# Reading x from two halves of a row in turns in a float32r up projection, with the output stored in two transfers

## The chip, the cores and the metric

The kernel runs on one core of a Trainium2 chip. The metric is the device time of one execution in microseconds; the time before is the median of three runs.

A core has a matrix engine (TensorE, PE in the profile; the loads of its stationary operand are listed as PEld), a vector engine (VectorE, DVE), an engine for activation functions (ScalarE, ACT), a general one (GpSimd, POOL) and SyncE (SP), which here issues nearly all DMAs. SBUF is the working memory, in 128 partitions; the matrix engine writes into PSUM.

## The reference

The first part is an mLSTM cell over 4 batches, 8 heads, 768 time steps and a head dimension of 40; the second a feed-forward block with the exact gelu on its output.

```python
for t in range(S):
    m_new = np.maximum(f_gate[:, :, t] + m, i_gate[:, :, t])
    f_stab = np.exp(f_gate[:, :, t] + m - m_new)
    i_stab = np.exp(i_gate[:, :, t] - m_new)
    m = m_new
    C = f_stab[:, :, None, None] * C + i_stab[:, :, None, None] * np.einsum('bhd,bhe->bhde', vt, kt)
    n = f_stab[:, :, None] * n + i_stab[:, :, None] * kt
    h_tilde = np.einsum('bhde,bhe->bhd', C, qt)
    denom = np.maximum(np.abs(np.einsum('bhd,bhd->bh', n, qt)[:, :, None]), 1.0)
    y[:, :, t] = h_tilde / denom / (1.0 + np.exp(-o_gate[:, :, t]))
x = y.transpose(0, 2, 1, 3).reshape(B * S, H * D)      # 3072 tokens x 320
h = x @ w_in                                           # 320 x 2048
g = 0.5 * h * (1.0 + erf(h / np.sqrt(2.0)))
out = g @ w_out                                        # 2048 x 320, 3072 rows
```

## The kernel before

**Chunks.** Time is cut into six chunks of 128 steps (`L`), and one chunk of all four batches makes 512 tokens (`TG`). For each chunk the class `Cell` computes the mLSTM output of each batch, and the feed-forward block follows: an up projection (`up_step` for chunk 0, `up` for chunks 1 to 5), the gelu, and a down projection (`first_down_steps`, `down_steps`). The down projection of chunk c is interleaved by hand with the cell of chunk c + 1: the strings `FRONT` and `DOWN` list the steps, a letter each, and `play` runs them in this order; the last chunk has no cell beside it. In `DOWN` an F is one piece of the down projection, X is `turn_y` and R is `split_x`.

**x.** `turn_y` transposes a finished batch into a PSUM tile px: 128 partitions by three groups (`NX + 1`) of 128 tokens. Groups 0 and 1 hold 128 features each; group 2 holds the last 64 features twice, once in each half of the partitions. For chunks 1 to 5 the projection is made in float32r (`F32R`) as three products, and x is stored as three parts: x_hi on ScalarE (L687), x_lo and x_all on VectorE in `split_x` (L700, L701). Each part is a tile of 128 partitions by three rows of 512 tokens, batch after batch; the 128 tokens of a batch stand in order in each row (`t`, a slice of 128 in all three rows).

**The up projection of chunks 1 to 5.** `up` has two rounds. Each round has two calls of `pair` and then `rest`. A `pair` makes 24 matmuls at L841: three products, two column blocks, two halves of the hidden width, two groups of features. The weights are the stationary operand (128 x 128), and one row of x, 128 partitions by 512 tokens, is the moving one; the result is a PSUM bank pu of 128 x 512. `rest` (L852) adds the last 64 features: 24 matmuls of 64 rows, whose two halves `e` use the upper and the lower 64 rows of the array. A chunk has so 96 matmuls of L841 and 48 of L852. ScalarE makes the gelu of each bank (L856) into `g.t`. Chunk 0 does the same in plain float32 with 256 columns (L786, L792).

**The down projection.** For chunks 1 to 5, `down_steps` uses a seven-product scheme on two halves of the tokens and of the hidden width; `hidden_sums` makes the sums it needs. Its matmuls (L922) have 128 tokens of one batch as the stationary operand, so the tokens of a batch come out as the partitions of a PSUM tile and of the output tile `o_sb`, in the order in which they stand in x.

**The stores.** `send` (L889) stores 128 rows of 320 float32 values of one batch with one DMA on SyncE. In a chunk of `down_steps`, `p3` sends batches 0 and 1, `p4` batches 2 and 3; in the last chunk `p4` runs for each of its two tiles by itself. SyncE's other transfers, the loads of q, k, v, the gates, M and the blocks of the next chunk, stand in the same queue in the order of the program.

Of the kernel before, what the change touches and what calls it, by code (L numbers as in the profile page):

```python
# [13 lines left out]
AF = mybir.ActivationFunctionType  # L14
OP = mybir.AluOpType

P = 128

I23 = 2.0 ** 23
PART = 1.0 - 2.0 ** -13  # L20
BASE = 1.0 + 2.0 ** -12
# [21 lines left out]
def kernel(  # L43
# [16 lines left out]
    nc = tc.nc  # L60

    B, H, S, D = q.shape
    L = P
    NCH = S // L
# [8 lines left out]
    R = P // 2  # L73
    NX = 2
# [59 lines left out]
    halves = (slice(0, R), slice(R, P))  # L134
# [8 lines left out]
    def load(n, first=0, end=4):  # L143

        if n >= NCH * B:
            return
        c, b = divmod(n, B)
        for src, dst in ((q, qb), (k, kb), (v, vb), (o_gate, None))[first:end]:
            if dst and swapped(c, b):
                x, to = src[b, :, c * L:(c + 1) * L, :].rearrange("h p d -> p h d"), dst[turn_of(n)][:, :, 0:D]  # L150
                for i in range(2):
                    nc.sync.dma_start(out=to[halves[i]], in_=x[halves[1 - i]])
                continue
            nc.sync.dma_start(out=dst[turn_of(n)][:, :, 0:D] if dst else out_of(n),  # L154
                              in_=src[b, :, c * L:(c + 1) * L, :].rearrange("h p d -> p h d"))
# [57 lines left out]
    a = gates.tile([BH, NCH, L], F32, name="a")  # L213
# [183 lines left out]
    def unread(bank):  # L397
        for _ in range(idle[0]):
            nc.tensor.matmul(bank, ident, ident, start=True, stop=True, skip_group_check=True)
        idle[0] = 0  # L400
# [3 lines left out]

    later_loads = []

    class Cell:


# [258 lines left out]
        def turn_y(self, b):  # L668
            n, t = self.c * B + b, slice(b * L, (b + 1) * L)
            if self.c > 0:  # L670
                px = ps_tr.tile([P, NX + 1, L], F32, name="px", tag="tr")
            else:
                px = ps_mm.tile([P, NX + 1, L], F32, name="px", tag="b")
            unread(px[:, 0, :])
            for k in range(NX + 1):
                y = ob[n % NLD][:, k * P:(k + 1) * P] if k < NX else y_rest.rearrange("p two r -> p (two r)")
                nc.tensor.transpose(px[:, k, :], y, ident)  # L677
            self.turned.append(b)
            if len(self.finished) > len(self.turned):
                self.twice(b + 1)  # L680
            if self.c == 0:
                nc.scalar.copy(out=first_x[:, :, t], in_=px)
                return
            self.px[b] = px
            if "x" not in parts:
                parts["x"] = raw.tile([P, NX + 1, TG], F32R, name="x_hi", tag="x", bufs=1)
            nc.scalar.activation(out=parts["x"][:, :, t], in_=px, func=AF.Copy, scale=PART)  # L687
            if self.c == 1 and b < NQ:
                load(n + NLD, 1, 3)
            if self.c == 1:  # L690
                load(n + NLD, 3, 4)
            else:
                later_loads.append(lambda: load(n + NLD, 3, 4))

        def split_x(self, b):
            px, t = self.px.pop(b), slice(b * L, (b + 1) * L)
            if b == 0:
                parts["x_lo"] = fars[0].tile([P, NX + 1, TG], F32R, name="x_lo", tag="x_lo", bufs=1)
            hi = parts["x"][:, :, t]
            nc.vector.scalar_tensor_tensor(out=parts["x_lo"][:, :, t], in0=px, scalar=-1.0 / BASE, in1=hi, op0=OP.mult, op1=OP.add)  # L700
            nc.vector.tensor_tensor(out=parts["x_all"][:, :, t], in0=px, in1=hi, op=OP.subtract)  # L701


    HF, HT, HD = NF // 2, TG // 2, DM // 2
# [9 lines left out]
    w_sums, parts, fars, w_hi, w_lo, w_mid = [], {}, [], [], [], {}  # L714
# [10 lines left out]
    def split_weight():  # L725
        i = len(w_lo)
        if i in (0, 3, 5, 8):
            two = shared([P, NX, 2, WP // 2], F32R, "w_in_hi")
            w_hi.extend([two[:, 0], two[:, 1]])
        elif i == 2:  # L730
            two = shared([P, 2, 2, WP // 2], F32R, "w_rest_hi")
            w_hi.append(two[:, 0])
            rest_two.append(two[:, 1])
        elif i == 7:
            w_hi.append(rest_two[0])
        w = w_all[i]
        nc.scalar.activation(out=w_hi[i], in_=w, func=AF.Copy, scale=PART * 2.0 ** -12)
        w_lo.append(w_f(F32R, "w_in_lo"))
        nc.vector.scalar_tensor_tensor(out=w_lo[i], in0=w_hi[i], scalar=-BASE * 2.0 ** 12, in1=w, op0=OP.mult, op1=OP.add)
# [3 lines left out]
    def join_weight(i):  # L743
        w_mid[i] = raw.tile([P, 2, WP // 2], F32R, name="w_in_mid", tag="pow") if i % 5 in (1, 4) else w_f(F32R, "w_mid")
        nc.vector.tensor_tensor(out=w_mid[i], in0=w_hi[i], in1=w_lo[i], op=OP.add)  # L745
# [74 lines left out]
    def up(g, sums_too, turns):  # L820

        def split_to(i):
            while len(w_lo) <= i:
                split_weight()

        def pair(f, ahead):

            at = [f // 2 * 5 + f % 2 * 3 + x for x in range(NX)]
            split_to(at[1])
            for i in at:  # L830
                if i not in w_mid:
                    join_weight(i)
            pus = [[pool.tile([P, TG], F32, name="pu", tag=tag) for e in range(2)]
                   for pool, tag in (((ps_h, "h"), (ps_mm, "a")), ((ps_tr, "tr"), (ps_mm, "b")))[f % 2]]
            ahead()
            mid = [w_mid.pop(i) for i in at]
            for n, (w, x) in enumerate((([w_hi[i] for i in at], parts["x"]), ([w_lo[i] for i in at], parts["x_lo"]), (mid, parts["x_all"]))):
                for i in range(2):
                    for e in range(2):
                        for k in range(NX):  # L840
                            nc.tensor.matmul(pus[i][e], w[k][:, e, i * P:(i + 1) * P], x[:, k, :],  # L841
                                             start=(n == 0 and k == 0), stop=False, skip_group_check=True)
            return pus

        def rest(u, banks, order):
            mid = w_mid.pop(5 * u + 2)
            for i in order:
                pu = banks[i]
                for n, (w, x) in enumerate(((w_hi[5 * u + 2], parts["x"]), (w_lo[5 * u + 2], parts["x_lo"]), (mid, parts["x_all"]))):
                    for e in range(2):  # L850
                        r = halves[e]
                        nc.tensor.matmul(pu[e], w[r, i // 2, i % 2 * P:(i % 2 + 1) * P], x[r, NX, :], start=False,  # L852
                                         stop=(n == 2), skip_group_check=True)

        def out(i, e, pu):
            nc.scalar.activation(out=g.t[:, HF * e + i, :], in_=pu[e], func=AF.Gelu, scale=4097.0)  # L856

        if c == 1:
            copy_chunk(2, range(1, B))
        b0 = pair(0, lambda: split_to(4))  # L860
        b1 = pair(1, lambda: join_weight(2))
        for step in turns[:1]:
            step()
        while later_loads:
            later_loads.pop(0)()
        if c == 1:
            copy_chunk(3)
        rest(0, b0 + b1, (0, 1, 2, 3))
        split_to(6)
        join_weight(5)  # L870
        join_weight(6)
        for i, pu in enumerate(b0 + b1):
            for e in range(2):
                out(i, e, pu)
        for step in sums_too[:5]:
            step()
        b2 = pair(2, lambda: split_to(9))
        hidden_sums(g, 0, 2)
        b3 = pair(3, lambda: (hidden_sums(g, 2, 4), join_weight(7)))
        for step in turns[1:] + sums_too[5:]:  # L880
            step()
        rest(1, b2 + b3, (2, 3, 0, 1))
        for i, e in ((2, 0), (2, 1), (3, 0), (0, 0), (1, 0), (3, 1), (0, 1), (1, 1)):
            out(4 + i, e, (b2 + b3)[i])
        hidden_sums(g, HF - 2, HF)
        hidden_sums(g, HF - 4, HF - 2)

    def send(c, b, o_sb):
        nc.sync.dma_start(out=out[b * S + c * L:b * S + (c + 1) * L, :], in_=o_sb)  # L889

    def first_down_steps(g):
        po = []
# [16 lines left out]
    def down_steps(c, g):  # L909
# [50 lines left out]
        def p3(pb):  # L960
            add(block(0, 1), pb, block(1, 0))
            for t in range(2):
                send(c, t, o_sb[0][:, t, :])
# [88 lines left out]
```

## Time and profile before

| | |
|---|---|
| time, median of 3 runs | 476.85 us (476.43 to 477.3) |
| span of the profiled execution, first to last instruction | 474.4 us |
| its own time beside the span | only the span is listed; it is 2.4 us under the median of the runs |
| PE busy, share of the span | 465.1 us, 98% |
| PEld, DVE, ACT, POOL busy | 403.4, 315.4, 238.2, 78.2 us |
| mean granted clock of TensorE | 1.000 |
| L841 in the chain that ended last | 24% |
| L852 in the chain that ended last | 6% |
| L922 in the chain that ended last | 33% |
| output stores (L889) | 24 of 160 KB, 1.9 us from issue to landing |

The busy time of PE is modelled from pipelined matmuls, each of which is listed longer than the distance to the next: L841's are listed at 387 to 633 ns. What one costs is read from the distance of their starts, or from a piece of the chain divided by its count. A few matmul records can be missing from a trace, so a piece of 24 can be listed as x23.

### The profile page before, as it was taken

Reading aid. Unit: us, or ns where it says so; the run is one execution under the profiler, and the core shown is the slowest. Engines: PE = TensorE matmul, PEld = TensorE weight load, DVE = VectorE, ACT = ScalarE, POOL = GpSimd, SP = SyncE. Lnnn points to the kernel's source line nnn. Section 1 sums busy time; section 2 is a strip of 40 time slices with the busy share of each in tenths; the row PEclk is TensorE's granted clock in tenths of the full one; section 3 lists DMA queues with packets and bytes.
Section 4 is the critical chain, followed back from the end, with each engine's and each line's share of the span. In section 5 each row is a group of like instructions: output and inputs, shape, how many; then the busy total and the mean of one; then the engine's idle time right before and its main releaser. Section 6 shows DMA issues by size and latency. Waiting matters only on the chain.

```text
span 474.4 us, 12960 instructions
## 1 busy us (share of the span) xinstructions
PE 465.1 (98%) x5380; PEld 403.4 (85%) x5380; DVE 315.4 (66%) x694; ACT 238.2 (50%) x517; POOL 78.2 (16%) x120
## 2 busy tenths in 40 slices
PE   7899999999999999999999999999999999999997
PEld 6787888877777899977899977899977899977997
DVE  7899789798869978635568645568647567624321
ACT  6986999844433873202873202873202882221300
POOL 3002020000030323200623200623102213000000
PEclk9999999999999999999999999999999999999999
DMA  9997992189845620359940359840339720100001
GB/s 175 184 233 180 184 245 72 59 196 197 181 120 117 98 55 3 65 143 208 130 82 3 61 145 186 146 90 3 57 74 224 116 48 3 57 1 0 1 1 55
DMA packets 172475, 49.79 MB, mean 105 GB/s; under 512 B 154400, under 2 KB 165952, under 8 KB 172416
## 3 DMA queue, kind: packets, MB, share of 16 engines
q1 hardware_dynamic: 172416, 48.97, 50.6%
q8 instruction: 42, 0.69, 0.6%
q14 instruction: 17, 0.14, 0.1%
HBM read 44.82 MB, written 9.37 MB: 114 GB/s over the span
## 4 chain that ended last, share of the span: by engine, by line
PE 93%; DVE 3%; SPq 1%; DMA 1%; issue 0%; ACT 0%; DVEq 0%
PE po L922 33%; PE pu L841 24%; PE po L899 7%; PE pu L852 6%; PE pu L786 6%; PE ph L637 4%; PE ps L535 3%; PE pu L792 2%; PE px L677 2%; PE pf L590 2%; SPq L154 1%; PE ps L519 1%; PE pf L601 1%; PE pf L557 1%; PE pt L497 1%; DMA bits<-in_moe_w_in_dram 1%
## 5 line engine op out<-in xcount | busy, mean ns | idle before, releaser
L856 ACT ACTIVATE g<-pu 128x512 f32<-128x512 f32 x80 | 40.8, 614 | 107.7 <-PE pu L852 107.6
L922 PE MATMUL po<-w_out,g 128*128 128x160 f32 x640 | 94.2, 302 | 0.0
L922 PEld LDWEIGHTS po<-w_out,g 128*128 128x128 f32 x640 | 87.8, 190 | 2.7 <-ACT g L856 1.8
L922 PE MATMUL po<-w_sums,sums 128*128 128x160 f32 x320 | 45.9, 302 | 0.0
L922 PEld LDWEIGHTS po<-w_sums,sums 128*128 128x128 f32 x320 | 43.8, 190 | 0.4
L841 PE MATMUL pu<-x_hi,w_in_hi 128*128 128x512 f32 x160 | 41.4, 400 | 0.0
L841 PE MATMUL pu<-x_lo,w_in_lo 128*128 128x512 f32 x160 | 40.6, 396 | 0.0
L447 ACT ACTIVATE W<-W,aT 128x128 f32<-128x128 f32 x128 | 39.2, 389 | 0.1
L421 POOL TENSOR_SCALAR_AFFINE_SELECT W<-W 128x1024 f32<-128x1024 f32 (+2 forms) x20 | 23.3, 1175 | 80.3 <-DMA W<-M_d 79.7
L841 PEld LDWEIGHTS pu<-x_hi,w_in_hi 128*128 128x128 f32 x160 | 29.4, 188 | 8.2 <-ACT g L856 1.9
L841 PEld LDWEIGHTS pu<-x_lo,w_in_lo 128*128 128x128 f32 x160 | 30.1, 188 | 7.2
L935 DVE TENSOR_TENSOR o_sb<-po,o_sb 128x320 f32<-128x320 f32 (+1 forms) x27 | 12.6, 466 | 34.2 <-PE po L922 30.2
L899 PE MATMUL po<-w_out,g 128*128 128x320 f32 x128 | 35.2, 433 | 0.0
L773 DVE TENSOR_TENSOR sums<-g 128x512 f32<-128x512 f32 x20 | 14.2, 710 | 30.4 <-ACT g L856 30.4
L745 DVE TENSOR_TENSOR w_in_mid<-w_in_hi,w_in_lo 128x512 fp32r<-128x512 f32 x20 | 13.8, 689 | 28.6 <-PE pu L841 28.6
L899 PEld LDWEIGHTS po<-w_out,g 128*128 128x128 f32 x128 | 24.0, 190 | 9.6
L666 ACT COPY y_rest<-ob 128x128 f32<-128x128 f32 x16 | 4.8, 298 | 54.1 <-DVE ob L659 31.0
L506 POOL TENSOR_TENSOR vw<-vb,ewT 128x328 f32<-128x328 f32 x12 | 9.1, 768 | 136.8 <-DMA vb<-in_v_dram 90.3
L841 PE MATMUL pu<-x_all,w_mid 128*128 128x512 f32 x80 | 31.6, 395 | 0.0
L841 PE MATMUL pu<-x_all,w_in_mid 128*128 128x512 f32 x80 | 31.6, 395 | 0.0
L786 PE MATMUL pu<-first_x,w_in 128*128 128x256 f32 x128 | 29.1, 382 | 0.0
L541 DVE TENSOR_TENSOR W<-ps,W 128x256 f32<-128x256 f32 (+1 forms) x48 | 18.1, 415 | 14.3 <-PE ps L535 11.9
(183 smaller groups left out, 879.5 us busy)
## 6 DMA issues: line engine op xcount, KB each, us to landing
W<-M_d SPq DMA_DIRECT2D x16, 512.0 KB, 5.8
bits<-in_moe_w_in_dram SPq DMA_DIRECT2D x20, 256.0 KB, 4.7
bits<-in_moe_w_out_dram SPq DMA_DIRECT2D x16, 320.0 KB, 3.2
blocks<-kq_d SPq DMA_DIRECT2D x32, 128.0 KB, 3.1
ob<-in_o_gate_dram SPq DMA_DIRECT2D x24, 160.0 KB, 4.1
out_dram<-o_sb SPq DMA_DIRECT2D x24, 160.0 KB, 1.9
kq_d<-in_k_dram SPq DMA_DIRECT2D x32, 80.0 KB, 2.4
kq_d<-in_q_dram SPq DMA_DIRECT2D x32, 80.0 KB, 2.4
```

What stands on the lines that cost most here:

```text
L421: nc.gpsimd.affine_select(out=x, in_=x, compare_op=OP.is_ge, fill=1.0e30, base=base, pattern=[[0, H], [1, x.shape[2]]], channel_multiplier=-1)
L447: nc.scalar.activation(out=W[n][:, h, :], in_=src, func=AF.Exp, scale=-1.0, bias=aT[:, self.c, r:r + 1])
L535: nc.tensor.matmul(ps[i][hip][halves[x ^ i], p, t], kT[i][r, p, halves[x]], qT[i][r, p, t], start=True, stop=True)
L541: nc.vector.tensor_tensor(out=w[r, :, t], in0=ps[i][hip][r, :, t], in1=w[r, :, t], op=OP.mult)
L637: nc.tensor.matmul(ph[r, h, :], Pm[:, h, r], vb[turn_of(n)][:, h, :], start=True, stop=True)
L773: nc.vector.tensor_tensor(out=s1, in0=a21, in1=a22, op=OP.add)
L786: nc.tensor.matmul(banks[-1][e][:, i - i0, :], in_tile(i, x)[:, e, i % 2 * P:(i % 2 + 1) * P], first_x[:, x, t0:t1], start=(x == 0 and i = ...
L841: nc.tensor.matmul(pus[i][e], w[k][:, e, i * P:(i + 1) * P], x[:, k, :], start=(n == 0 and k == 0), stop=False, skip_group_check=True)
L852: nc.tensor.matmul(pu[e], w[r, i // 2, i % 2 * P:(i % 2 + 1) * P], x[r, NX, :], start=False, stop=(n == 2), skip_group_check=True)
L856: nc.scalar.activation(out=g.t[:, HF * e + i, :], in_=pu[e], func=AF.Gelu, scale=4097.0)
L899: nc.tensor.matmul(po[b], g.t[:, f, b * L:(b + 1) * L], w_out[:, f, :], start=(f == 0), stop=(f == NF - 1))
L922: nc.tensor.matmul(bank[at][:, i, :], lhs(j, t), rhs(j), start=(first and i == 0 and j == 0), stop=(i == n - 1 and j == HF - 1), skip_grou ...
```

## The change

The token order within a row of x changes, and with it three other places.

- x is stored by token halves. A row of 512 holds first the tokens 0 to 63 of all four batches, then the tokens 64 to 127 of all four (`in_place`; `by_set` views px in the same way). L687, L700 and L701 write through these views.
- The matmuls at L841 and L852 read a row in turns: element 0, element 256, element 1, element 257 and so on (`in_turns`). The result is written to the bank in one run (`in_pairs` only gives it the same shape). Column 2i + a of a batch in pu is so token 64a + i of the batch.
- The rows of `o_sb` of chunks 1 to 5 come in that order too. `send` stores the even partitions as the tokens 0 to 63 and the odd ones as 64 to 127, with two DMAs. Both are on SyncE, but in the last chunk the second is issued on ScalarE.

Chunk 0 keeps its layout, its matmuls and its stores.

```diff
+    def by_set(px):
+        return px.rearrange("p k (a i) -> p (k a) i", a=2)
+    def in_place(x, b):
+        return x.rearrange("p k (a t) -> p (k a) t", a=2)[:, :, b * R:(b + 1) * R]
+    def in_turns(x):
+        return x.rearrange("p (a t) -> p t a", a=2)
+    def in_pairs(pu):
+        return pu.rearrange("p (t a) -> p t a", a=2)
...
-            nc.scalar.activation(out=parts["x"][:, :, t], in_=px, func=AF.Copy, scale=PART)
+            nc.scalar.activation(out=in_place(parts["x"], b), in_=by_set(px), func=AF.Copy, scale=PART)
...
-            px, t = self.px.pop(b), slice(b * L, (b + 1) * L)
+            px = by_set(self.px.pop(b))
...
-            hi = parts["x"][:, :, t]
-            nc.vector.scalar_tensor_tensor(out=parts["x_lo"][:, :, t], in0=px, scalar=-1.0 / BASE, in1=hi, op0=OP.mult, op1=OP.add)
-            nc.vector.tensor_tensor(out=parts["x_all"][:, :, t], in0=px, in1=hi, op=OP.subtract)
+            hi = in_place(parts["x"], b)
+            nc.vector.scalar_tensor_tensor(out=in_place(parts["x_lo"], b), in0=px, scalar=-1.0 / BASE, in1=hi, op0=OP.mult, op1=OP.add)
+            nc.vector.tensor_tensor(out=in_place(parts["x_all"], b), in0=px, in1=hi, op=OP.subtract)
...
-                            nc.tensor.matmul(pus[i][e], w[k][:, e, i * P:(i + 1) * P], x[:, k, :],
+                            nc.tensor.matmul(in_pairs(pus[i][e]), w[k][:, e, i * P:(i + 1) * P], in_turns(x[:, k, :]),
                                              start=(n == 0 and k == 0), stop=False, skip_group_check=True)
...
-                        nc.tensor.matmul(pu[e], w[r, i // 2, i % 2 * P:(i % 2 + 1) * P], x[r, NX, :], start=False,
+                        nc.tensor.matmul(in_pairs(pu[e]), w[r, i // 2, i % 2 * P:(i % 2 + 1) * P], in_turns(x[r, NX, :]), start=False,
                                          stop=(n == 2), skip_group_check=True)
...
     def send(c, b, o_sb):
-        nc.sync.dma_start(out=out[b * S + c * L:b * S + (c + 1) * L, :], in_=o_sb)
+        to = out[b * S + c * L:b * S + (c + 1) * L, :]
+        if c == 0:
+            nc.sync.dma_start(out=to, in_=o_sb)
+            return
+        for a in range(2):
+            queue = nc.scalar if a and c == NCH - 1 else nc.sync
+            queue.dma_start(out=to[halves[a]], in_=o_sb[a::2])
```

## The prediction

> **What bounds the kernel now.** I read the page first (busy time and the chain of waits), then the chain in order of time, then single matmuls in the timeline, and last the busy time of the other engines around them.
>
> ```profile
> PE 465.1 (98%) x5380; PEld 403.4 (85%) x5380; DVE 315.4 (66%) x694; ACT 238.2 (50%) x517; POOL 78.2 (16%) x120
> ...
> PE 93%; DVE 3%; SPq 1%; DMA 1%; issue 0%; ACT 0%; DVEq 0%
> PE po L922 33%; PE pu L841 24%; PE po L899 7%; PE pu L852 6%; PE pu L786 6%; PE ph L637 4%; PE ps L535 3%; PE pu L792 2%; PE px L677 2%; PE pf L590 2%; SPq L154 1%; PE ps L519 1%; PE pf L601 1%; PE pf L557 1%; PE pt L497 1%; DMA bits<-in_moe_w_in_dram 1%
> ```
>
> TensorE (PE) is the chain: 93% of the span, and from about 54 us on it hardly stops. Whatever changes PE's own time per matmul changes the total almost one for one; what other engines do counts only if it makes PE wait. L841 and L852, the later chunks' up projection that the change touches, are 24% and 6% of the span.
>
> Now the price of one such matmul. The chain in order of time, columns start us, length us, what:
>
> ```profile
> 53.92 6.91 PE pu L786 x32
> 60.83 1.93 PE pu L792 x16
> ...
> 64.53 3.46 PE pu L786 x16
> 67.98 1.06 PE pu L792 x8
> ...
> 412.12 11.16 PE pu L841 x48
> 423.29 2.99 PE pu L852 x23
> 426.27 11.38 PE pu L841 x48
> 437.65 2.99 PE pu L852 x24
> 440.64 30.64 PE po L922 x224
> ```
>
> L786 is the first chunk's up projection: float32, 256 columns, 6.91 / 32 = 215.9 ns each, so a float32 column costs 0.84 ns. L841 runs 512 columns of float32r: 11.16 / 48 = 232.5 ns each, 0.45 ns a column. If float32r were exactly twice as fast a column as float32, 512 of its columns would take the 215.9 ns of 256 float32 ones. They take 16.6 ns more. The same shows in the rest rows (64 rows, two matmuls side by side on the two halves of the array): L792 gives (1.93 - 1.06) / 4 = 0.2175 us for each pair, with 0.19 us once for getting in and out (1.06 - 4 x 0.2175); for the 12 pairs of L852 that would be 2.80 us, and they take 2.99.
>
> Is that excess a disturbance by other engines? The timeline of a stretch in which they are still (start, length, instruction), and two rows of the busy time by stretches (from:to in us, length, busy us of PE, PEld, VectorE, ScalarE, GpSimd with their instructions, granted clock, DMA share, GB/s):
>
> ```profile
> 430.02 0.39 PE L841 MATMUL pu<-x_all,w_mid 128*128 128x512 f32 x1
> 430.26 0.40 PE L841 MATMUL pu<-x_all,w_in_mid 128*128 128x512 f32 x1
> 430.49 0.39 PE L841 MATMUL pu<-x_all,w_mid 128*128 128x512 f32 x1
> 430.72 0.39 PE L841 MATMUL pu<-x_all,w_in_mid 128*128 128x512 f32 x1
> ...
> 53.92:60.83 6.91, 6.91 (x35) 5.80 (x33) 4.19 (x8) 6.84 (x14) 1.09 (x1) 1.00 0.97 190
> 429.20:431.80 2.60, 2.60 (x13) 2.10 (x12) 0.00 (x0) 0.00 (x0) 0.00 (x0) 1.00 0.00 0
> ```
>
> The last row is decisive: from 429.20 to 431.80 VectorE, ScalarE, GpSimd and the DMAs do nothing and the granted clock is 1.00, and yet matmuls start 0.23 to 0.24 us apart. In the float32 stretch of 53.92 to 60.83 ScalarE is busy throughout and the DMAs at 97%, and the spacing is 215.9. So the excess belongs to how PE takes a float32r matmul. What differs from the float32 rows is the rate at which the moving operand, x, must come out of SBUF: 0.42 ns an element at the floor against 0.84. That points to the reading of x, whose order the change alters. The trace can't tell whether it is the order in a row or a collision with the weight loads (188 ns of every 232).
>
> **The change, part by part.**
>
> *Order of reading x (L841, L852).* Before: 512 elements in a row. After: one from the first 1 KB of a row, one from the second, in turns. No matmul of the trace reads like that, so the price has two bounds. Below: 215.9 ns, the float32 row's spacing; a column can't beat half of a float32 column if the pace of the columns is the limit there. Gain: 480 matmuls of L841 x 16.6 ns = 8.0 us, and 10 rest stages x (2.99 - 2.80) = 1.9 us; together 9.9. Above: each element costs what a float32 column costs, 0.84 ns, so 432 ns a matmul or pair: 600 x (432 - 232.5) = 119.7 us more. I take the lower bound: two streams 1 KB apart let the fetch of one fall beside the use of the other, the row that it is nearest to is the float32 one where the fetch keeps up, and the existing price stands only 16.6 ns above it but 200 below the other.
>
> [...]
>
> *Writing the product.* The columns of pu are written in the same run of addresses as before: nothing. Which token a column stands for changes, but the four batches stay 128 columns each, so the down projection and the sums of hidden halves are unaltered in number and shape.
>
> *Storing x.* L687, L700 and L701 write the same 384 elements a batch, in runs of 64 instead of 128. They take 485, 552 and 549 ns. The cover: in the border at 271.8 us the last batch's x_hi is written from 269.63 to 270.12, x_lo to 270.71, x_all to 271.18; PE reads x_hi from 271.77, x_lo eight matmuls (1.9 us) later, x_all eight after that. If the shorter runs doubled all three, x_hi would end 0.5 us later and the other two about 1.6, still in time: nothing. Without that cover it would cost 0.5 us a chunk.
>
> *Storing the output.* 20 stores become 40 of half the rows. In chunks 1 to 4 that is 16 more issues on SP, 0.33 to 0.53 us each, so 1.3 to 2.1 us a chunk. Queued behind them on SP are the loads of blocks, W, k, v and the gate for the next chunk. SP waits 152 us in all for o_sb at L889, so the time is there; what is late by up to 2 us is for instance W, issued from 285.22 to 289.48 and masked on GpSimd from 297.25 to 300.10, while ScalarE starts on it only after the gelus, at about 302.4. I count nothing; exposed in full it would be 4 x 1.3 to 4 x 2.1, 5 to 8 us. In the last chunk half of the stores go over ScalarE's queue, which has only finished copies before it. The last store was issued at 471.65 and the end waited for its landing, 1.35 us; two halves issued together cost between -0.3 us (less to move) and +0.5 (a second issue of 0.33 that comes late, or a slower first use of that queue). I take nothing.
>
> *What comes late next.* With up 2 us shorter a chunk, the gelus must still feed the down projection. ScalarE runs each in 0.61 us and starts them as the rest products finish, so they shift with PE. SP has 2 us less for its loads in each up, which adds to the 2 above.
>
> **The sum.** The span is 474.4 us, 2.4 below the median of 476.85, and I keep that difference. 474.4 - 9.9 = 464.5 in the trace, 476.85 - 9.9 = 467.0 in the measured time.
>
> **The rivals.**
>
> *Part of the excess stays* (chance 0.23). Weight loads still share the memory with x. Spacings in L841 come down to 224 ns where the other engines interfere, so a value between is reachable: (232.5 - 224) x 600 = 5.1 us, 471.8.
>
> *The order makes no difference to PE* (0.17). For it: the excess may be the weight loads' alone, and those don't change; a repeat of 231, 232, 237 ns in the still stretch is the same for all tiles of x. Against: float32 matmuls load as many weights in as short a time and pay nothing. Then only the stores remain, 0 to 2 us of loads that come late where the cover is thin: 476.9 to 479.
>
> *Each element from another place costs a float32 column* (0.19). One mechanism, at L841 and L852: x can't be fetched two elements at a time once neighbours in time aren't neighbours in memory. 476.85 + 119.7 = 596.6 us. It decides from 233 ns a matmul on; already 256 ns would be 600 x 23.5 = 14 us more. For it: the float32 row shows PE taking 0.84 ns an element as an ordinary rate. Against it: nothing in the trace, which has no strided moving operand at all.
>
> **How the numbers follow.** Full removal 0.41, partial 0.23 (less 0.01 for a part too small to see), no difference 0.17 (0.07 within 0.2% of before, 0.10 slower), half rate 0.19. 0.2% is about what a measurement here can tell from no change, some 1 us. Faster 0.63, same 0.08, slower 0.29. Leaving out the half rate alone leaves 0.81: from 467.0 less the tail's 0.3 and the runs' own 0.4 to 0.9 (465.8) up to the 479 of the second rival. The likeliest case by itself reaches from 465.8 to 468.5, with the partial one to 472.
>
> **What would show it.** Right: L841 starts near 216 ns apart, its pieces in the chain of waits fall from 11.16 to about 10.4 us, those of L852 from 2.99 to 2.8, and L922 stays at 4.54 for 32. PE should still be 98% busy, with no new waits on W or blocks. Wrong: L841 at 232 (the excess comes from elsewhere), at some 430 (the fetch halves), or PE idle at the borders behind loads that SP issued late.

## The result and the profile after

The changed kernel takes 469.16 us (median; 468.34 to 470.64) against 476.64 us in the same comparison: a ratio of 0.9834, 95% interval 0.9803 to 0.9865. Timed again on another occasion it gave 468.99 us, ratio 0.9842 (0.9820 to 0.9864). It is 7.5 us faster; 9.9 were forecast. The time lies within the forecast's range, 2.2 us above the 467.0 of its sum and 0.7 us above the 468.5 that the likeliest case was given by itself.

The chain of waits of the changed kernel, in order of time, for the last chunk (start us, length us, what; L860 is the former L841, L871 the former L852, L947 the former L922):

```profile
408.19 10.36 PE pu L860 x48
418.55 2.79 PE pu L871 x24
421.34 10.56 PE pu L860 x48
431.90 2.79 PE pu L871 x24
434.68 30.64 PE po L947 x224
```

10.36 / 48 = 215.8 ns a matmul. The whole excess of 16.6 ns over the float32 row is gone, and the pairs of the rest have come from 2.99 to 2.79 us a stage, so one up projection takes 26.50 us instead of 28.52. The down projection behind it is unchanged at 30.64. Five chunks give 5 x 2.02 = 10.1 us.

Three lines of the timeline in a stretch where the other engines are as still as in the one shown of before, and the row of the busy time by stretches for it:

```profile
424.83 0.38 PE L860 MATMUL pu<-x_all,w_mid 128*128 128x512 f32 x1
425.04 0.38 PE L860 MATMUL pu<-x_all,w_in_mid 128*128 128x512 f32 x1
425.26 0.38 PE L860 MATMUL pu<-x_all,w_mid 128*128 128x512 f32 x1
...
424.20:426.80 2.60, 2.60 (x14) 2.28 (x13) 0.05 (x1) 0.00 (x0) 0.00 (x0) 1.00 0.00 0
```

Starts are now 0.21 to 0.22 us apart where they were 0.23 to 0.24. The pattern 231, 232, 237 is gone; in every tile of x and every chunk the median is 216.

So 10.1 us were gained and 7.5 arrived. The rest went in two places, both behind the stores. First, PE waits for the blocks of the next chunk. The chain of waits of the changed kernel around 240 us, with some pieces left out:

```profile
234.86 2.10 SPq L170
...
237.00 3.06 DMA blocks<-kq_d
...
240.18 0.71 DVE kT L488
...
246.50 1.40 PE ps L554 x41
```

The line of before for the same matmuls (its L535 is the L554 of now), and a line of the list of waits of the changed kernel (total us, times, longest us):

```profile
247.22 1.50 PE ps L535 x64
```

```profile
DVE kT L488 <- DMA blocks<-kq_d: 3.4, 2, 2.4
```

In before the chain runs through PE alone here, and its list of waits has none of kT for blocks. Now the chain leaves PE: SyncE issues the loads of blocks late (L170), they land at 240.06, the transposes kT and qT follow, and PE's scores (L554) start late. Matched by position in the program, PE's matmuls lose 1.2 us on those of before between 235 and 251 us, and 0.55 us between 312 and 320. Second, the tail, from PE's last end to the end of the span, is 3.54 us instead of 3.16. Together 2.1 us: 10.1 - 2.1 = 8.0.

The profiled execution lost 2.4 us more ahead of 131 us, where nothing is changed: 1.5 us of it between 15 and 19 us, where PE's granted clock was 0.61 (15 to 17 us) and 0.69 (17 to 20 us) against 1.00 in before (mean 0.996 over the span). This comes and goes with the execution: the other three of this kernel had clock 1.000 and spans of 466.6 to 467.8 us, near the 474.4 - 8.0 = 466.4 that the sum asks for, and executions of before with 0.996 occur too.

### The profile page after: what moved, and what is told of

Its sections match the earlier page's. It is cut to its first block, busy times and chain, and to the rows that moved or that the text cites. A ratio compares the mean times of both kernels' runs of the same rounds, so it can differ in the third digit from the quotient of the medians.

```text
span 468.8 us, 12989 instructions
## 1 busy us (share of the span) xinstructions
PE 458.0 (98%) x5380; PEld 406.4 (87%) x5380; DVE 319.9 (68%) x694; ACT 238.1 (51%) x517; POOL 79.8 (17%) x120
## 4 chain that ended last, share of the span: by engine, by line
PE 87%; DVE 7%; DMA 2%; issue 1%; SPq 1%; ACT 1%; DVEq 0%
PE po L947 31%; PE pu L860 22%; PE po L924 7%; PE pu L871 6%; PE pu L805 5%; PE ph L656 3%; PE ps L554 2%; PE ps L538 2%; PE px L696 2%; PE pu L811 2%; PE pf L609 1%; DMA kb<-in_k_dram 1%; PE pf L620 1%; SPq L170 1%; PE pt L516 1%
## 5 line engine op out<-in xcount | busy, mean ns | idle before, releaser
L947 PE MATMUL po<-w_out,g 128*128 128x160 f32 x640 | 94.2, 302 | 0.0
L947 PEld LDWEIGHTS po<-w_out,g 128*128 128x128 f32 x640 | 87.8, 190 | 2.5 <-ACT g L875 1.7
L947 PE MATMUL po<-w_sums,sums 128*128 128x160 f32 x320 | 45.9, 302 | 0.0
L947 PEld LDWEIGHTS po<-w_sums,sums 128*128 128x128 f32 x320 | 43.8, 190 | 0.4
L860 PE MATMUL pu<-x_hi,w_in_hi 128*128 128x512 f32 x160 | 39.0, 386 | 0.0
L440 POOL TENSOR_SCALAR_AFFINE_SELECT W<-W 128x1024 f32<-128x1024 f32 (+2 forms) x20 | 24.7, 1245 | 81.6 <-DMA W<-M_d 81.1
L860 PE MATMUL pu<-x_lo,w_in_lo 128*128 128x512 f32 x160 | 37.8, 379 | 0.0
L860 PEld LDWEIGHTS pu<-x_hi,w_in_hi 128*128 128x128 f32 x160 | 29.6, 189 | 5.6 <-ACT g L875 1.7
L792 DVE TENSOR_TENSOR sums<-g 128x512 f32<-128x512 f32 x20 | 16.4, 820 | 26.5 <-ACT g L875 26.5
L860 PEld LDWEIGHTS pu<-x_lo,w_in_lo 128*128 128x128 f32 x160 | 30.2, 189 | 4.3
L860 PE MATMUL pu<-x_all,w_mid 128*128 128x512 f32 x80 | 30.3, 379 | 0.0
L860 PE MATMUL pu<-x_all,w_in_mid 128*128 128x512 f32 x80 | 30.3, 379 | 0.0
L805 PEld LDWEIGHTS pu<-first_x,w_in 128*128 128x128 f32 x128 | 23.8, 190 | 4.3 <-DVE w_in L387 1.0
```

Of the source, the lines that this page charges most:

```text
L440: nc.gpsimd.affine_select(out=x, in_=x, compare_op=OP.is_ge, fill=1.0e30, base=base, pattern=[[0, H], [1, x.shape[2]]], channel_multiplier=-1)
L792: nc.vector.tensor_tensor(out=s1, in0=a21, in1=a22, op=OP.add)
L805: nc.tensor.matmul(banks[-1][e][:, i - i0, :], in_tile(i, x)[:, e, i % 2 * P:(i % 2 + 1) * P], first_x[:, x, t0:t1], start=(x == 0 and i = ...
L860: nc.tensor.matmul(in_pairs(pus[i][e]), w[k][:, e, i * P:(i + 1) * P], in_turns(x[:, k, :]), start=(n == 0 and k == 0), stop=False, skip_g ...
L947: nc.tensor.matmul(bank[at][:, i, :], lhs(j, t), rhs(j), start=(first and i == 0 and j == 0), stop=(i == n - 1 and j == HF - 1), skip_grou ...
```

## The experiments

**The changed kernel again**, beside the next three.

> The changed kernel unaltered, timed beside the others on one chip. Its up projection gave 9.8 us (49 pieces of 0.8 us and 0.2 us), but its profile was only 5.6 us shorter: 2.2 us were lost ahead of 131 us, where nothing is changed, 1.2 us at 247 us and some 0.5 us at 316 us, where PE waits for blocks, and 0.3 us at the end. If the 2.2 us were chance, its median should be 468 to 469 us and the trace's first up projection should start near 129.3 us; if they belong to the change, again near 131.7 us.

Measured: 468.99 us. In its trace PE again loses 1.0 us at 247 us, 0.7 us at 318 us, and the tail is 3.53 us. The first up projection again starts late in the profiled execution, 1.4 us after that of before, and its granted clock is again 0.996; the other three, with clocks of 0.999 and 1.000, have spans of 467.1 to 467.3. Little or nothing of the late start thus belongs to the change; why both profiled executions had it stays open.

**Two stores alone.** The kernel before, with nothing but this:

```diff
-        nc.sync.dma_start(out=out[b * S + c * L:b * S + (c + 1) * L, :], in_=o_sb)
+        to = out[b * S + c * L:b * S + (c + 1) * L, :]
+        if c == 0:
+            nc.sync.dma_start(out=to, in_=o_sb)
+            return
+        for a in range(2):
+            queue = nc.scalar if a and c == NCH - 1 else nc.sync
+            queue.dma_start(out=to[halves[a]], in_=o_sb[halves[a]])
```

> The kernel before, with the stores of chunks 1 to 5 split in two (rows 0 to 63 and 64 to 127), and nothing else. Theory: the 16 extra issues on SyncE push the loads of blocks back, so PE waits for them at about 250 us as in the changed kernel: 1 to 2 us slower than before, 477.8 to 478.8 us. Rival: the loads have room as long as the up projection is long, and only its shortening exposes them: no difference, 476.3 to 477.0 us.

Measured: 477.89 against 476.38 us, ratio 1.0033 (1.0018 to 1.0048): 1.5 us slower, at the lower end of the first theory's 477.8 to 478.8. PE loses 0.4 us at 250 us and 0.5 at 316, and the tail is 3.69 us, 0.5 more. The extra stores cost time even while the up projection is long. The wait at 250 us is 0.4 here and 1.2 in the changed kernel, so the shorter up projection makes this one longer: the rival has a part.

**One store, all else as changed.**

```diff
-        if c == 0:
-            nc.sync.dma_start(out=to, in_=o_sb)
-            return
-        for a in range(2):
-            queue = nc.scalar if a and c == NCH - 1 else nc.sync
-            queue.dma_start(out=to[halves[a]], in_=o_sb[a::2])
+        nc.sync.dma_start(out=to, in_=o_sb)
```

> The changed kernel with one store per batch, as before; the output rows of chunks 1 to 5 stay in the order in which the matmuls leave them, so they aren't the reference's rows. Theory (the extra issues cost the 1.7 us of waits and the 0.3 us at the end): 2 us less than the changed kernel, 466.7 to 467.2 us, no wait at 247 us. Rival (the shorter up projection exposes the loads): the same as the changed kernel, with the wait for blocks still there.

Measured: 466.66 us, ratio 0.9789 (0.9766 to 0.9812), 2.3 us less than the changed kernel beside it. PE doesn't wait for blocks at 247 us or at 316, and the tail is 3.16 us again. This is the lower edge of the theory's 466.7 to 467.2, and it is within 0.4 us of the forecast of 467.0, which had counted the stores at nothing. How SyncE's issues stand, from the timeline of before and then of the changed kernel (start us, length us, x how many):

```profile
195.82 0.83 SPq L889 DMA_DIRECT2D out_dram<-o_sb  x2
228.83 7.40 SPq L170 DMA_DIRECT2D blocks<-kq_d  x8
```

```profile
196.19 2.48 SPq L914 DMA_DIRECT2D out_dram<-o_sb  x4
233.28 7.49 SPq L170 DMA_DIRECT2D blocks<-kq_d  x8
```

Two batches took SyncE 0.83 us and now take 2.48, because the issue of a half is also longer than that of a whole. The lines for it in the view of o_sb, before and after (min/median/max ns):

```profile
L889 SPq DMA_DIRECT2D out_dram<-o_sb x24: 332/388/528, 128.5 to 471.7; - x24
```

```profile
L914 SPq DMA_DIRECT2D out_dram<-o_sb x36: 471/594/682, 196.2 to 465.7; - x36
```

The loads of blocks started 28.6 us after the up projection's start in before (228.83 - 200.24) and start 32.7 us after it now (233.28 - 200.60): 4.1 us later by the clock of PE's work. 3.1 us of it is the longer issue of the two groups of stores in front of them (0.83 to 2.48 us, and 1.00 to 2.45 for the second). The shorter up projection accounts for little: with one store the loads start 29.4 us after it (227.52 - 198.17). At the end, the second half lands on ScalarE's queue 2.12 us after its issue starts, where the whole store took 1.77.

**The order made in the transposes.** The same reading of x, but even tokens in the first half of a row and odd ones in the second, so that the product's rows come out in their natural order and one store is enough:

```diff
-                nc.tensor.transpose(px[:, k, :], y, ident)
+                nc.tensor.transpose(px[:, k, :] if self.c == 0 else px[:, k, :].rearrange("p (a i) -> p a i", a=2), y,
+                                    ident if self.c == 0 else ident.rearrange("p (i a) -> p a i", a=2))
...
-        if c == 0:
-            nc.sync.dma_start(out=to, in_=o_sb)
-            return
-        for a in range(2):
-            queue = nc.scalar if a and c == NCH - 1 else nc.sync
-            queue.dma_start(out=to[halves[a]], in_=o_sb[a::2])
+        nc.sync.dma_start(out=to, in_=o_sb)
```

> The changed kernel, but the tokens are put in halves by the transposes of x (the identity's columns read two apart), even tokens in the first half of a row and odd in the second, so that the product's rows come out in their natural order and one store per batch is enough. Theory: as the kernel with one store, 466.7 to 467.2 us; the 60 transposes may cost up to 0.1 us each if a moving operand with step two is read at half the pace, 6 us at most, some 473 us. Rival: no better than the changed kernel, 468 to 469 us.

Measured: 466.21 us (465.79 to 467.17), ratio 0.9784 (0.9761 to 0.9807), 10.2 us faster than before and 2.8 faster than the changed kernel. A group of three transposes has gone from 0.33 to 0.34 or 0.35 us. This version gives the reference's rows and beats both the kernel before and the changed one; from the 466.66 of the kernel with one store it can't be told apart.

**The second store on ScalarE in all chunks.**

```diff
-            queue = nc.scalar if a and c == NCH - 1 else nc.sync
+            queue = nc.scalar if a else nc.sync
```

> The changed kernel with the second store of each batch of chunks 1 to 5 issued on ScalarE, not only in the last chunk. Theory (the waits at 247 and 316 us come from SyncE's time for the extra issues, 0.6 us each ahead of the loads): they go, 1.7 us less than the changed kernel, 467.2 to 467.6 us, if ScalarE has room for 16 issues and for waiting on the additions of VectorE. Rival 1: ScalarE, which stands in its own order, waits at each store and delays the gelus or the weights W: 469 us or more. Rival 2 (the smaller transfers themselves crowd the loads): no change, 468.9 us.

Measured: 480.33 us, ratio 1.0081 (1.0052 to 1.0109): slower than before. This is the first rival. The timeline of ScalarE around the stores (ACTq is its queue of DMA issues):

```profile
196.03 1.21 ACTq L914 DMA_DIRECT2D out_dram<-o_sb  x2
197.28 0.22 ACT L671 ACTIVATE den<-qb 128x8 f32<-128x8 f32 x1 [3.26 <-issue]
```

ScalarE stood still for 3.26 us, its stores waiting for VectorE's addition, and with it the abs of the last batch (L671), on which that batch's x and the next up projection depend. This happens at all four borders between chunks 1 to 5 (3.26 us once, 3.19 three times), and PE loses 2.9, 2.8, 2.3 and 3.9 us there on before. Around 250 us, where the changed kernel loses 1.2 us on before, this one gains 0.6, and around 316 it loses 0.1 instead of 0.55, so moving the issues off SyncE does relieve the blocks, as the theory has it, but at a higher price. A part of the 11 us to the changed kernel lies in the clock: from 414.7 to 418.0 us, right behind PE's wait at the last border, the granted clock was 0.50, and a piece of 16 matmuls of L947 took 3.56 us there instead of 2.17. All seven executions have a mean clock of 0.989 to 0.996; how much of their time that makes was not separated.

**Which orders of reading x are free.** Four runs of one execution each, all at a granted clock of 1.000. The order at L841 and L852 is another one in each chunk (in the last run two chunks have fewer weights instead); the kernel is otherwise the one before. The former L841 is L860, L861 or L866 in these runs. The shape of the edit:

```diff
+    def streams(x, a):
+        return x.rearrange("p (a t) -> p t a", a=a)          # a streams, one element each
+    def apart(x, d):
+        return x.rearrange("p (g a t) -> p g t a", a=2, t=d)   # two streams d elements apart
+    def grains(x, t):
+        return x.rearrange("p (a g t) -> p g a t", a=2, t=t)   # t elements from each half
...
-                            nc.tensor.matmul(pus[i][e], w[k][:, e, i * P:(i + 1) * P], x[:, k, :],
+                            moving = ORDER[c](x[:, k, :])
+                            nc.tensor.matmul(like(pus[i][e], moving), w[k][:, e, i * P:(i + 1) * P], moving,
```

> The kernel before, with another order of reading x in the float32r up projection of each chunk: 4, 16, 64, 128 and 256 streams in chunks 1 to 5, one element from each in turn, so that one element and the next are 512, 128, 32, 16 and 8 bytes apart. The output's rows are in another order and not the reference's. Theory A (two reads in a row from one small piece of memory collide; any order that keeps neighbours in time far apart is free of it): 216 ns a matmul for 4 and 16 streams, rising to 232 or more where the distance gets small. Theory B (only two streams fit what the engine holds): 216 for none, more than 232 for 4 and above, up to 432. [...]

The chain's pieces for the first round of chunks 1, 2 and 5 (4, 16 and 256 streams):

```profile
128.92 13.34 PE pu L860 x48
...
205.21 20.90 PE pu L860 x48
...
492.20 21.71 PE pu L860 x48
```

Starts are 272 to 283 ns apart with 4 streams, 435 with 16, 431 with 64, 461 with 128 and 453 with 256, the last being a walk in steps of two. Theory A's 216 for 4 and 16 streams is wrong. Theory B came close, though 16, 128 and 256 exceed its 432. All five orders are slower than the plain row's 232, which the two streams of the changed kernel, at 216, are not. The half rate that the forecast priced as a rival exists, then, from 16 streams on (431 to 461 ns), only not for two streams.

> The kernel before, with x read from two streams that are 128, 32, 8, 4 and 2 elements apart in chunks 1 to 5 (512, 128, 32, 16, 8 bytes). The output's rows are in another order and not the reference's. Theory A: 216 ns a matmul as long as the two are in different pieces of memory, 232 or more below some distance, at the latest at 8 bytes. Theory C (the distance doesn't matter, breaking the run of neighbouring addresses does): 216 ns for all five.

Chunks 4 and 5, two streams 16 and 8 bytes apart:

```profile
336.53 10.36 PE pu L860 x48
...
403.95 11.16 PE pu L860 x48
```

The spacing is 216 ns down to a distance of 16 bytes, and at 8 bytes exactly the 232 of the plain row; these are theory A's values. So the two halves needn't be 1 KB apart, which takes away the picture in the forecast of two far regions of memory, and breaking the run isn't enough either (theory C).

> The kernel before, with x read from the two halves of a row in turns of 2, 4, 8, 32 and 128 elements in chunks 1 to 5, where the changed kernel has turns of 1. The output's rows are in another order and not the reference's. Theory A: at turns of 2 or 4 neighbours in time share a piece of 8 or 16 bytes and the collision is back: 232 ns from some small turn on. Rival: the excess is paid at each border of a longer piece, so turns up to that piece's size stay at 216, and 32 or 128 come to 232.

Turns of 2, of 4 and of 128:

```profile
128.87 15.71 PE pu L860 x48
...
211.44 12.16 PE pu L860 x48
...
427.01 11.16 PE pu L860 x48
```

Turns of 2, 4, 8, 32 and 128 give 327, 254, 243, 236 and 232 ns: theory A is right that the excess returns, but not in its size; a turn of 2 or 4 is worse than the plain row.

> The kernel before with less to read, results meaningless in chunks 1 to 5: chunk 1 reads one element of x again and again, chunk 2 each of 256 elements twice running, chunk 3 the same 256 elements in a row two times; chunks 4 and 5 read x as before but load only 64 and 32 weight columns in two of the three products (32 of 48 matmuls). If the fetch of x is the limit: chunks 1 and 2 at 216 ns, chunk 3 at 232, chunks 4 and 5 at 232. If the excess is a collision with the loading of weights: chunk 3 at 232, chunk 4 near 224 and chunk 5 near 220 in the two narrow products, and chunk 1 at 216 only if a repeated read isn't made again.

One element again and again, one row of 256 read twice, and the two with fewer weights (chunks 1, 3, 4 and 5):

```profile
129.14 10.36 PE pu L861 x48
...
267.63 11.16 PE pu L861 x48
...
338.84 11.08 PE pu L861 x48
...
408.12 11.13 PE pu L861 x48
```

Each of 256 elements twice running also gave 216. With a half or a quarter of the weight columns loaded in two of three products, a weight load there is listed at 134 or 108 ns instead of 188, and yet the spacing is 231 to 233 ns on average instead of 233 to 234. The excess hardly depends on the weight loads; it depends on the order of x. That settles what the forecast left open.

**A picture of two lanes, tried on new orders.** Most of these fit if PE takes successive elements in two lanes, odd reads in one and even reads in the other, and if a lane keeps pace (216 ns) while its own reads stay in one piece of 16 bytes, called a line here, for four reads, loses some 8% (232) with two, and half (431 to 461) with one. This is an estimate from the spacings above; the 16 bytes are four elements and come from two streams at 16 bytes (216 ns) and at 8 (232). In a plain row each lane takes every other element, two of a line; with two streams each lane walks one stream, four of a line. Not all of them fit: with four streams a lane changes lines at every read and takes only 277 ns, and in turns of 4, 8 and 32 a lane reads two of a line, as in a plain row, but takes 254, 243 and 236 ns. What a change between far lines costs a lane is thus not in the picture.

> Other orders of reading x again, results meaningless in chunks 1 to 5. The runs so far fit a picture of two lanes: odd and even reads are fetched apart, and a lane keeps pace when its own successive reads stay in a line of 16 bytes for four of them, loses 8% with two, and half with one. Chunk 1: two streams, each element twice running (A0 A0 B0 B0 A1 A1 ..): by the lanes each lane now changes between two lines at every read, as with four streams, 271 to 283 ns; without lanes, two lines held at once, as with two streams, 216 ns. Chunk 2: eight streams, one element each; chunk 3: four streams, each element twice: by the lanes the same time for both, between 283 and 435 ns; without lanes chunk 3 would take what four streams took, 271 to 283. Chunk 4: every second element of a row, each twice: by the lanes 232. Chunk 5: every fourth element, each twice: by the lanes 435 to 461.

The first round of each of chunks 1 to 5:

```profile
129.55 13.46 PE pu L866 x48
...
205.96 23.36 PE pu L866 x48
...
307.75 23.36 PE pu L866 x48
...
409.47 11.18 PE pu L866 x48
...
478.93 21.72 PE pu L866 x48
```

Two streams with each element twice cost what four streams cost (13.46 against 13.34), not the 10.36 of two streams. Eight streams and four streams with each element twice are the same to the last digit. Every second element twice is the plain row (232), and every fourth twice equals the walk in steps of two (21.72 against 21.71), in which the odd lane makes the very same reads. All four equalities of the picture hold. One number was missed: eight streams take 487 ns, not between 283 and 435, more than sixteen take; the picture says nothing of how lines lie in memory, and that stays open.

## Why the prediction was right, point by point

**The bound and the excess.** Right: PE sets the end, and 16.6 ns a matmul of L841 were there to gain whatever the other engines do. It gave 10.1 us against the 9.9 of the sum.

**The reason for the lower bound.** The value was right and its reason was not shown. That "two streams 1 KB apart let the fetch of one fall beside the use of the other" was the author's estimate: no run shows a fetch by itself, and the 1 KB has no part in it, since 16 bytes do (216 ns, against 232 at 8 bytes). A change of place at each read costs nothing by itself here: two streams make one at every read and run at 216 ns. That the existing price stood near one bound and far from the other was no argument at all; four streams lie between them at 277, and eight at 487 lie above the upper one, so 432 wasn't an upper bound either. That the changed kernel uses exactly two streams, the one number of those tried (2, 4, 8, 16 and more) that is free, was in this sense luck.

**Product and storing of x.** It cost nothing, as said: ScalarE's x_hi takes 484 ns, VectorE's two parts 551 and 547, against 485, 552 and 549.

**Storing the output.** This is the term that was mis-sized: counted at nothing, it cost 2.3 us (468.99 against 466.66). The step that failed is "SP waits 152 us in all for o_sb at L889, so the time is there". The time was there as a sum, not at the place: 61 of the 152 us lie in the last chunk, and nearly all of the rest is one wait of 22 to 23 us in each chunk, ahead of its first store, so it leaves no room for what comes behind the stores (in the changed kernel it is still 21 to 23 us). What counts is the queue behind the stores, loads that fill the up projection without a gap and end with the blocks. Also, the issue was sized from those of whole stores (0.33 to 0.53 us), and halves take 0.47 to 0.68, so a chunk has 3.1 us more, not 1.3 to 2.1. The example looked at was W, and its cover did not hold either. ScalarE now waits for the W that GpSimd masks (L440), 0.6 us at 231 us and 1.3 at 302, which it does neither in before nor with one store:

```profile
ACT W L466 <- POOL W L440: 1.9, 2, 1.3
```

SyncE in turn waits up to 1.3 us for ScalarE's W before it issues a load that stands ahead of the blocks. So "no new waits on W or blocks", which the prediction gave as a sign of being right, failed for both, and only the blocks were seen to reach PE. Of the cases that the prediction priced, the second rival alone had the stores at more than nothing, 0 to 2 us. The tail's bound of -0.3 to +0.5 us holds the 0.4 measured.

**What comes late next.** "SP has 2 us less for its loads in each up" was seen and not priced. It fits the runs: the wait at 250 us is 0.4 us with the stores alone, 1.2 with both, and none with the shorter up projection alone.

**The rivals.** A part of the excess staying, no difference, and the float32 price all fall for this order. The half rate is real for others (431 to 487 ns with 8 to 256 streams). The total came to stand where the prediction had only the partial case, between 468.5 and 472, but not for its reason: the excess went whole, and the stores took a part back.

## What to carry to other kernels

A float32r matmul that reads a plain row loses 16.6 ns of 232 here; reading two streams 16 bytes to 1 KB apart in turns took that away (216 ns), and four or more streams cost far more than they save (277 to 487 ns). Make such an order where it is free, in the transpose that writes the operand, so that the results leave in their own order and nothing has to be undone in the stores. A queue's total idle time says nothing of what an added transfer will delay: follow each transfer behind it to the engine that waits, and take the time of an issue from one of the same size.

## What the runs showed of the hardware

- A float32r matmul of 512 columns took 216 ns with x read from two streams 16 bytes to 1 KB apart, 232 from a plain row or two streams 8 bytes apart, 277 from four streams, 431 to 487 from 8 to 256, and 327 to 236 in turns of 2 to 32 elements. The order, not only the amount, set the pace. The picture of two lanes with lines of 16 bytes fits 216, 232 and 431 to 487 as four, two and one reads of a line in a row; the four streams and the turns lie outside it. It is inferred from these prices and the equalities above; nothing showed the lanes directly.
- A store of 64 rows took SyncE longer to issue (median 594 ns from every second partition, 592 from adjacent ones) than one of 128 (388 ns), and landed no earlier at the end: 2.12 us on ScalarE's queue and 1.84 on SyncE's, against 1.77.
